# Storing silu's derivative instead of its argument, in the forward pass of a training kernel

## The chip, the cores and the metric

The kernel runs on one core of one Trainium2 chip. The metric is the device time of one execution in microseconds. Three runs of the kernel before gave 873.41, 874.69 and 877.84 us; the median is 874.69 us.

## The reference

One layer of a network and its whole gradient. With B = 1, L = 2048 positions, D = 512 channels, N = 128 states and a hidden width F = 1792, all in bf16:

```python
xn = layernorm(x)
K  = einsum("dn,dnl,dn->dl", C, exp(dt*A*l), dt*B).real     # 2048 taps for each channel
s  = causal_conv(xn, K) + xn * Dskip                        # by FFT in the reference
h  = xn @ w1;  o = silu(h) @ w2                             # 512 -> 1792 -> 512
g  = silu(o)
out = x + s * g
```

The kernel returns `out` and, for a given `grad_out`, the gradients of x, of the six state-space parameters, of log_dt, of Dskip, and of w1 and w2. The two silus matter here. The backward needs their derivatives: the gradient that reaches o is `grad_out * s * silu'(o)`, and the gradient that reaches h is `(do @ w2^T) * silu'(h)`.

## The kernel before

The program is written out by hand in six stages. Each engine works through its own instructions in the order in which the Python code issues them, so the order on ScalarE (ACT) is what the code says, and one instruction that waits holds up all behind it.

**Stage 1** (up to about 197 us) does the forward feed-forward part, and beside it builds tables for the convolution and powers of the state matrix. The generator `gen_ffn_fwd` runs over four groups of 512 positions (`tc_`), and in each over seven pairs of column blocks of w1 (`f0`), 28 steps in all. A step computes two 128x512 blocks of h into a PSUM tile `ps_h` (8 matmuls, L557), and ACT reads that tile twice: once for silu(h) into `aT` (L559), once for a plain copy of h as bf16 into `hs` (L560), which goes to DRAM as `hTd`. The PSUM pool that holds `ps_h` (`pd`) has two buffers, shared with another matmul result (`ps_m`). The previous group's second product is interleaved: `gen_o` accumulates o in `ps_o` (L533) for one block of 128 positions at a time, 16 in all, and for each ACT stores silu(o) into `g2` and a copy of o into `o2` (both through the helper `later`, so the profile shows them on its line, L76). They go to DRAM as `gd` and `od`. In the same steps, from a hand-made list of ticks, ACT computes `Abs` and `Sin` for the transform tables (`tb_w`, `tb_f`, L374 to L378) and for the powers (`b_w`, `b_s`, L465 to L467), and copies PSUM results (`tb_m`, `tb_i`, `XNT`). Near the end of the stage ACT copies the powers into place (`X`, `Y`, `CY`, L720) once they have come back from DRAM as `XYc`.

**Stages 2 to 5** build the kernel K, transform it, do the convolution and its gradient, and the gradients of w2 and of the parameters. In stages 3 and 4, `YOut` loads `od`, `gd`, x and grad_out for two blocks of 128 positions at a time. `pre` applies silu's derivative to the loaded o in place, by the helper `DSILU` (ACT, L133), and multiplies grad_out by it (VectorE, DVE, L1173). `out` then forms the output and the gradient `DO`.

**Stage 6** (from about 680 us) is the feed-forward part's backward. `Bwd.dh` runs over 28 steps. It loads a pair of h blocks (`hsb`, three buffers, asked for three steps ahead), computes silu's derivative of them on ACT into `sd` (L133), eight matmuls of the gradient (`ps_da`, L1626), and on DVE the product of both into `dhT` (L1627). Transposes of `dhT` (L1648), copied out by ACT (L1650), go to DRAM for w1's gradient. `dx` does the second product (L1665) and the layer norm's gradient one step behind.

ACT evaluates functions from tables. The built program has an instruction that loads a table set where the next function isn't in the set that is loaded (`ACT_TABLE_LOAD` in the profile). Before, there are four in the whole program: for exp at the start, for silu at the first L559, for silu's derivative at the first use of L133, and for exp in the last stage. The copies, `Abs` and `Sin` of stage 1 run under silu's set without a load of their own.

The places that the change touches are L537 (the copy of o in `gen_o`), L560, L1172 (in `pre`) and L1620 to L1627 (in `dh`).

Of the kernel before, what the change touches and what calls it, by code (L numbers as in the profile page):

```python
# [9 lines left out]
ALU = mybir.AluOpType  # L10
F32 = mybir.dt.float32
BF16 = mybir.dt.bfloat16
I32 = mybir.dt.int32
AX = mybir.AxisListType
P = 128
# [51 lines left out]
def later(k, fn, *a, **kw):  # L67

    k.after.append((fn, a, kw))


def settle(k):

    todo, k.after = k.after, []
    for fn, a, kw in todo:
        fn(*a, **kw)  # L76
# [55 lines left out]
def DSILU(nc, pool, out, in_):  # L132
    nc.scalar.activation(out=out, in_=in_, func=ACT.Derivative_silu)  # L133
# [364 lines left out]
def gen_ffn_fwd(k, fs, W1, W2):  # L498

    nc = k.nc  # L500

    def xnt(tc_):
        XNT = fs.tile([P, DK, 4, P], BF16, name="XNT", tag="XNT")
        for h in range(2):
            pt = k.ps.tile([P, 2, 4, P], BF16, name="pt_x", tag="ps")
            for d_ in range(2):
                for t in range(4):
                    dk = 2 * h + d_
                    nc.tensor.transpose(out=pt[:, d_, t, :], in_=k.xn[:, 4 * tc_ + t, dk * P:(dk + 1) * P], identity=k.ident[:])
            (nc.scalar.copy if h else nc.vector.tensor_copy)(out=XNT[:, 2 * h:2 * h + 2], in_=pt[:])  # L510
        return XNT

    def trans(tc_, aT, f0):
        pt = k.ps.tile([P, 2, 4, P], BF16, name="pt_a", tag="ps")
        for j in range(2):
            for t in range(4):
                nc.tensor.transpose(out=pt[:, j, t, :], in_=aT[:, f0 + j, t * P:(t + 1) * P], identity=k.ident[:])
        ak = fs.tile([P, 2, 4, P], BF16, name="ak", tag="ak", bufs=3)
        later(k, nc.vector.tensor_copy, out=ak[:], in_=pt[:])
        later(k, nc.sync.dma_start, k.akd[f0:f0 + 2, :, 4 * tc_:4 * tc_ + 4].rearrange("f p t q -> p f t q"), ak[:])  # L520

    def gen_o(tc_, aT):
        for th in range(2):
            ts_ = slice(4 * tc_ + 2 * th, 4 * tc_ + 2 * th + 2)
            g2 = fs.tile([P, 2, D], BF16, name="g2", tag="g2", bufs=1)
            o2 = fs.tile([P, 2, D], BF16, name="o2", tag="o2", bufs=1)
            G2 = fs.tile([P, 2, D], BF16, name="G2", tag="G2", bufs=1)
            nc.sync.dma_start(G2[:], k.g_v[:, ts_, :])
            for t in range(2):
                tt = 2 * th + t  # L530
                pso = k.ps.tile([P, D], F32, name="ps_o", tag="ps")
                for ft in range(FT):
                    nc.tensor.matmul(out=pso[:], lhsT=aT[:, ft, tt * P:(tt + 1) * P], rhs=W2[:, ft, :], start=(ft == 0), stop=(ft == FT - 1))  # L533
                    if ft == FT // 2 - 1:
                        yield
                later(k, nc.scalar.activation, out=g2[:, t, :], in_=pso[:], func=ACT.Silu)
                later(k, nc.scalar.copy, out=o2[:, t, :], in_=pso[:])  # L537
                if t == 0:
                    yield
            later(k, nc.sync.dma_start, k.tl(k.gd[:])[:, ts_, :], g2[:])  # L540
            later(k, nc.sync.dma_start, k.tl(k.od[:])[:, ts_, :], o2[:])
            later(k, later, k, nc.vector.tensor_tensor, out=k.DS[:, ts_, :], in0=G2[:], in1=g2[:], op=ALU.mult)
            yield

    prev = iter(())
    XNT = xnt(0)
    late = None
    for tc_ in range(4):
        aT = fs.tile([P, FT, 512], BF16, name="aT", tag="aT")
        nxt = None  # L550
        for f0 in range(0, FT, 2):
            yield
            ps = k.pd.tile([P, 2, 512], F32, name="ps_h", tag="pd")
            for j in range(2):
                ft = f0 + j
                for dk in range(DK):
                    nc.tensor.matmul(out=ps[:, j], lhsT=W1[:, dk, ft * P:(ft + 1) * P], rhs=XNT[:, dk], start=(dk == 0), stop=(dk == DK - 1))  # L557
            hs = fs.tile([P, 2, 512], BF16, name="hs", tag="hs", bufs=3)
            nc.scalar.activation(out=aT[:, f0:f0 + 2, :], in_=ps[:], func=ACT.Silu)  # L559
            nc.scalar.copy(out=hs[:], in_=ps[:])  # L560
            nc.sync.dma_start(k.hTd[tc_][:, f0:f0 + 2], hs[:])
            next(prev, None)
            if f0 == FT - 2:
                next(prev, None)
            k.mid()
            if late:
                trans(*late)
            late = (tc_, aT, f0)
            if f0 == FT - 4 and tc_ < 3:
                settle(k)  # L570
                nxt = xnt(tc_ + 1)
        XNT = nxt
        prev = gen_o(tc_, aT)
    yield
    trans(*late)
    k.last_aT = aT
    for _ in prev:
        k.mid()
        yield
# [13 lines left out]
def stage_1(k):  # L593
# [14 lines left out]
    su.norm(0)  # L608
    k.mid = lambda: None
    gf = gen_ffn_fwd(k, fs, W1, W2)  # L610
    early = {1: lambda: (su.stats(1), su.norm(1)), 2: lambda: su.param(1), 3: lambda: (su.stats(2), su.norm(2)),
             4: lambda: (su.param(2), su.param(3)), 5: lambda: (su.stats(3), su.norm(3)), 6: lambda: (su.param(4), su.param(5))}
# [538 lines left out]
class YOut:  # L1151
# [17 lines left out]
    def pre(self, t0):  # L1169

        k, nc, r = self.k, self.k.nc, self.ins[t0]
        DSILU(nc, k.y2, r["co"][:], r["co"][:])  # L1172
        nc.vector.tensor_tensor(out=r["cG"][:], in0=r["cG"][:], in1=r["co"][:], op=ALU.mult)  # L1173

    def out(self, t0, S_s):
# [414 lines left out]
class Bwd:  # L1590
# [23 lines left out]
    def dh(self, n):  # L1614
        k, nc = self.k, self.k.nc
        tc_, f0 = n // 7, 2 * (n % 7)
        if f0 == 0:
            self.dhT = self.fb.tile([P, FT, 512], BF16, name="dhT", tag="dhT")
        hs = self.hs.pop(n)
        sd = self.fw.tile([P, 2, 512], BF16, name="sd", tag="sd")  # L1620
        DSILU(nc, self.fw, sd[:], hs[:])
        ps = k.pd.tile([P, 2, 512], F32, name="ps_da", tag="pd")
        for j in range(2):
            ft = f0 + j
            for dk in range(DK):
                nc.tensor.matmul(out=ps[:, j], lhsT=self.W2T[:, dk, ft * P:(ft + 1) * P], rhs=self.DOT[tc_][:, dk], start=(dk == 0), stop=(dk == DK - 1))  # L1626
        nc.vector.tensor_tensor(out=self.dhT[:, f0:f0 + 2, :], in0=ps[:], in1=sd[:], op=ALU.mult)  # L1627
        if n + 3 < 28:
            self.ld_h(n + 3)
        self.trans()  # L1630
        self.late = (tc_, self.dhT, f0)
# [161 lines left out]
```

## Time and profile before

| what | us |
|---|---|
| median of three runs | 874.69 |
| the profiled execution | 874.37 |
| its span in the trace | 872.6 |
| PE (matmuls) busy | 676.4 (78%) |
| DVE busy | 632.0 (72%) |
| ACT busy | 450.6 (52%) |
| POOL busy | 47.6 (5%) |

The times of instructions in the text are from the start of that span. A group of instructions is named by its line, engine, operation and tiles ("out<-in"); "idle before" is the time that the engine stood still just before such an instruction, and the name behind the arrow is what ended it. The chain is the sequence of work and waits that ended last, followed back from the end. The share of busy time is an average over stages that have different limits, so the text reads stretches of the span one by one.

### The profile page before, as it was taken

The numbers are of one execution on the slowest core, as the hardware profiler recorded it, in microseconds if no ns is written. First come the engines' busy times: TensorE is split into PE (matmuls) and PEld (weight loads), VectorE is DVE, ScalarE is ACT, GpSimd is POOL, SyncE is SP. The second block draws the span as 40 slices with busy tenths as digits, with TensorE's granted clock in tenths as the row PEclk, the third lists the DMA queues.
The fourth block names the chain that finished last, engine by engine and source line by source line (L and its number), as shares of the span: only waits on it lengthen the run. The fifth ranks groups of instructions, "written<-read, shape, count | busy, mean of one in ns | idle before, by whom it ended". The sixth has DMA issues, their size and how long they took to land.

```text
span 872.6 us, 13569 instructions
## 1 busy us (share of the span) xinstructions
PE 676.4 (78%) x5213; PEld 346.3 (40%) x5284; DVE 632.0 (72%) x1005; ACT 450.6 (52%) x547; POOL 47.6 (5%) x49
## 2 busy tenths in 40 slices
PE   5677886957557739766879399598688699999966
PEld 2334443423445536322334144243233355555433
DVE  6898888757999962997988999266264347776850
ACT  4459999854879835342444022054244376664231
POOL 1254221000000000000000001000000000000000
PEclk9988997987868859998989799799898899999988
DMA  9547767777769677784788685999879595668362
GB/s 273 175 149 242 266 223 257 264 250 211 217 221 305 187 195 251 266 337 148 259 333 279 209 330 209 253 250 248 208 187 205 146 224 165 177 187 277 98 202 67
DMA packets 183952, 195.18 MB, mean 224 GB/s; under 512 B 35659, under 2 KB 147791, under 8 KB 178767
## 3 DMA queue, kind: packets, MB, share of 16 engines
q1 hardware_dynamic: 179310, 185.53, 69.6%
q10 hardware_dynamic: 4577, 8.77, 3.4%
q8 instruction: 41, 0.67, 0.3%
q14 instruction: 24, 0.20, 0.1%
HBM read 110.10 MB, written 80.50 MB: 218 GB/s over the span
## 4 chain that ended last, share of the span: by engine, by line
PE 36%; DVE 28%; DMA 16%; ACT 9%; issue 6%; SPq 3%; POOL 0%; ACTq 0%; DVEq 0%; POOLq 0%
PE ps_v L1038 7%; DMA XTl<-XTd 5%; PE ps_da L1626 5%; PE ps_dx L1665 4%; PE ps_f L1014 4%; PE ps_w L1744 2%; PE ps_h L557 2%; DMA AW<-akd 2%; PE ps_w L1381 2%; DMA out_dram<-o10b 2%; DVE cm_t L106 2%; PE ps_o L533 1%; PE pt_dh L1648 1%; DVE m L747 1%; PE ps_f L894 1%
## 5 line engine op out<-in xcount | busy, mean ns | idle before, releaser
L1038 PEld LDWEIGHTS <-TIs 128*128 128x128 bf16 x384 | 39.7, 104 | 85.0 <-issue 37.8
L557 PE MATMUL ps_h<-XNT,W 128*128 128x512 bf16 x212 | 61.1, 432 | 14.7 <-ACT hs L560 13.7
L1744 PE MATMUL ps_w<-dhc,xn 128*128 128x448 bf16 x256 | 53.5, 371 | 6.9 <-ACT o10b L1746 6.9
L1531 DVE TENSOR_TENSOR T<-Vb,YTl 128x2048 bf16<-128x2048 bf16 x16 | 19.6, 1225 | 53.5 <-ACT Vb L1522 53.4
L1627 DVE TENSOR_TENSOR dhT<-ps_da,sd 128x1024 bf16<-128x1024 f32 x28 | 34.2, 1224 | 32.7 <-ACT sd L133 19.3
L1014 PEld LDWEIGHTS <-TFs 128*128 128x128 bf16 x336 | 32.9, 100 | 62.0 <-DMA TFs<-TFd 15.4
L1626 PE MATMUL ps_da<-DOT,W2T 128*128 128x512 bf16 x218 | 53.3, 384 | 2.3 <-ACT DOT L1606 1.9
L533 PE MATMUL ps_o<-W,aT 128*128 128x512 bf16 x221 | 53.1, 386 | 0.2
L1381 PE MATMUL ps_w<-DO_all,AW 128*128 128x512 bf16 x212 | 51.5, 388 | 1.9 <-issue 1.8
L1665 PE MATMUL ps_dx<-W1T,dhT 128*128 128x512 bf16 x215 | 52.0, 379 | 0.4
L855 ACT COPY XT<-pt_xt 128x1024 bf16<-128x1024 bf16 (+1 forms) x44 | 41.2, 1010 | 21.5 <-DMA K_b<-Kud 10.1
L1014 PE MATMUL ps_f<-DS,TFs 128*128 128x512 bf16 x173 | 43.3, 400 | 11.2 <-DMA TFs<-TFd 9.5
L894 PE MATMUL ps_f<-xn,TFs 128*128 128x512 bf16 x120 | 36.5, 456 | 16.9 <-ACT XU L895 15.8
L853 PE MATMUL pt_xt<-ident_bfloat,X 128*128 128x128 bf16 x328 | 29.9, 251 | 23.0 <-ACT XT L855 13.4
L1522 ACT CAST Vb<-ps_V 128x1024 bf16<-128x1024 f32 x32 | 31.7, 1013 | 28.9 <-PE ps_V L1520 21.8
L1038 PE MATMUL ps_v<-BG,TIs 128*128 128x512 bf16 x123 | 34.5, 436 | 11.9 <-DMA TIs<-TId 9.4
L1014 PE MATMUL ps_f<-K_b,TFs 128*128 128x512 bf16 x156 | 36.5, 379 | 8.8 <-ACT Ak L1016 5.1
L1038 PE MATMUL ps_v<-BK,TIs 128*128 128x512 bf16 x126 | 31.5, 404 | 13.6 <-DVE BK L97 13.5
L1744 PEld LDWEIGHTS <-xn 128*128 128x128 bf16 x256 | 26.1, 102 | 37.6 <-issue 11.1
L557 PEld LDWEIGHTS <-W 128*128 128x128 bf16 x224 | 23.3, 108 | 41.0 <-issue 25.4
L853 PEld LDWEIGHTS <-X 128*128 128x128 bf16 x328 | 25.3, 114 | 27.2 <-issue 25.4
L452 POOL TENSOR_TENSOR ex<-ex 128x512 f32<-128x512 f32 x21 | 33.0, 1582 | 53.1 <-DVE XYg L480 28.1
(287 smaller groups left out, 1457.9 us busy)
## 6 DMA issues: line engine op xcount, KB each, us to landing
TFs<-TFd SPq DMA_DIRECT2D x12, 1024.0 KB
TIs<-TId SPq DMA_DIRECT2D x24, 512.0 KB
XTd<-XT SPq DMA_DIRECT2D x20, 512.0 KB
XTl<-XTd SPq DMA_DIRECT2D x16, 640.0 KB
UXl<-UXd SPq DMA_DIRECT2D x8, 1024.0 KB
hTd<-hs SPq DMA_DIRECT2D x28, 256.0 KB
akd<-ak SPq DMA_DIRECT2D x28, 256.0 KB
AW<-akd ACTq DMA_DIRECT2D x14, 512.0 KB
```

Source lines behind the costliest of these rows:

```text
L533: nc.tensor.matmul(out=pso[:], lhsT=aT[:, ft, tt * P:(tt + 1) * P], rhs=W2[:, ft, :], start=(ft == 0), stop=(ft == FT - 1))
L557: nc.tensor.matmul(out=ps[:, j], lhsT=W1[:, dk, ft * P:(ft + 1) * P], rhs=XNT[:, dk], start=(dk == 0), stop=(dk == DK - 1))
L853: nc.tensor.transpose(out=pt[:, j, c], in_=X[:, c, P * kk:P * kk + P], identity=k.ident[:])
L855: nc.scalar.copy(out=XT[:, j0:j0 + len(ks)], in_=pt[:, 0:len(ks)])
L894: nc.tensor.matmul(out=ps[:, c, :], lhsT=TFs[:, t1 + 4 * j, c, :], rhs=src[:, t1 + 4 * j, :], start=(j == 0), stop=(j == 3))
L1014: nc.tensor.matmul(out=ps[:, c, :], lhsT=tab(j), rhs=src[:, t1 + 4 * j, :], start=(n == 0), stop=(n == 4 * len(terms) - 1))
L1038: nc.tensor.matmul(out=ps[:, j, :], lhsT=TIs[:, j, 2 * kt + c, :], rhs=B[kt][:, c, (t0 + j) % 4, :], start=(kt == 0 and c == 0), stop=(kt ...
L1381: nc.tensor.matmul(out=ps[:], lhsT=A[:, t, :], rhs=k.DO[:, t, :], start=(t == 0), stop=(t == T - 1))
L1626: nc.tensor.matmul(out=ps[:, j], lhsT=self.W2T[:, dk, ft * P:(ft + 1) * P], rhs=self.DOT[tc_][:, dk], start=(dk == 0), stop=(dk == DK - 1))
L1627: nc.vector.tensor_tensor(out=self.dhT[:, f0:f0 + 2, :], in0=ps[:], in1=sd[:], op=ALU.mult)
L1665: nc.tensor.matmul(out=psx[:], lhsT=dhT[:, ft, t % 4 * P:(t % 4 + 1) * P], rhs=self.W1T[:, ft, :], start=(ft == 0), stop=(ft == FT - 1))
L1744: nc.tensor.matmul(out=ps[:], lhsT=k.xn[:, t, dk * P:(dk + 1) * P], rhs=ch[i][:, t, :], start=(t == 0), stop=(t == T - 1))
```

## The change

The forward stores the derivative where it stored the argument. In the 28 steps on h, ACT reads `ps_h` once for silu and once for silu's derivative, and `hTd` then holds silu'(h). In the 16 blocks of o it does the same, and `od` holds silu'(o). The backward loads these and multiplies by them: 28 instructions on ACT in stage 6 and 8 in stages 3 and 4 are gone, with the tile `sd`. Shapes, types, sizes of transfers, buffers and the order of everything else stay as they were.

In the built program silu and its derivative are in different table sets, and so a load stands ahead of every silu and of every derivative in stage 1: there are 90 `ACT_TABLE_LOAD`s in place of 4. `Abs`, `Sin` and the copies run under either set and need none.

```diff
                 later(k, nc.scalar.activation, out=g2[:, t, :], in_=pso[:], func=ACT.Silu)
-                later(k, nc.scalar.copy, out=o2[:, t, :], in_=pso[:])
+                later(k, DSILU, nc, fs, o2[:, t, :], pso[:])
...
             nc.scalar.activation(out=aT[:, f0:f0 + 2, :], in_=ps[:], func=ACT.Silu)
-            nc.scalar.copy(out=hs[:], in_=ps[:])
+            DSILU(nc, fs, hs[:], ps[:])
...
         k, nc, r = self.k, self.k.nc, self.ins[t0]
-        DSILU(nc, k.y2, r["co"][:], r["co"][:])
         nc.vector.tensor_tensor(out=r["cG"][:], in0=r["cG"][:], in1=r["co"][:], op=ALU.mult)
...
         hs = self.hs.pop(n)
-        sd = self.fw.tile([P, 2, 512], BF16, name="sd", tag="sd")
-        DSILU(nc, self.fw, sd[:], hs[:])
...
-        nc.vector.tensor_tensor(out=self.dhT[:, f0:f0 + 2, :], in0=ps[:], in1=sd[:], op=ALU.mult)
+        nc.vector.tensor_tensor(out=self.dhT[:, f0:f0 + 2, :], in0=ps[:], in1=hs[:], op=ALU.mult)
```

## The prediction

> **What bounds the kernel now.** The change touches ACT in stage 1 (it adds work there) and in stages 3, 4 and 6 (it takes work away). I first asked the stretches of stage 1 how busy each engine is. The stage runs from the first silu at 16.41 us to the first copy of the next stage at 197.03 us.
>
> ```profile
> core 0: us, PE busy (x) PEld busy (x) DVE busy (x) ACT busy (x) POOL busy (x), PEclk, DMA share, GB/s
> 16.41:40.40 23.99, 16.71 (x125) 9.57 (x126) 19.05 (x47) 12.49 (x14) 6.33 (x10) 0.93 0.65 212
> 40.40:64.34 23.94, 19.01 (x116) 10.10 (x117) 23.56 (x50) 14.81 (x19) 10.98 (x7) 0.85 0.41 143
> 64.34:174.66 110.32, 89.08 (x582) 47.81 (x593) 93.20 (x114) 102.47 (x128) 23.50 (x19) 0.92 0.72 248
> 174.66:197.03 22.37, 11.99 (x55) 5.39 (x55) 11.95 (x21) 13.71 (x19) 0.00 (x0) 0.86 0.79 251
> 16.41:197.03 180.62, 136.80 (x874) 72.88 (x889) 147.76 (x229) 143.47 (x178) 40.81 (x35) 0.91 0.68 230
> ```
>
> ACT is free for 37.15 of 180.62 us, but for 7.85 of 110.32 us in the long third stretch: there ACT is the fullest engine, and what is added to it lengthens the stage. In the second stretch DVE is the full one (23.56 of 23.94). The share of ACT over the whole span, 52%, hides this.
>
> The groups of instructions on ACT give the prices, and the timeline shows how a table load stands between two instructions:
>
> ```profile
> L133 ACT ACTIVATE sd<-hsb 128x1024 bf16<-128x1024 bf16 x28 | 29.3, 1050 | 8.0 <-DMA hsb<-hTd 8.0
> L559 ACT ACTIVATE aT<-ps_h 128x1024 bf16<-128x1024 f32 x28 | 29.1, 1040 | 12.5 <-PE ps_h L557 12.3
> L560 ACT CAST hs<-ps_h 128x1024 bf16<-128x1024 f32 x28 | 28.9, 1032 | 2.3 <-DMA hTd<-hs 2.3
> L76 ACT CAST o<-ps_o 128x512 bf16<-128x512 f32 x16 | 10.1, 632 | 0.0
> L559 ACT ACT_TABLE_LOAD x1 | 1.3, 1283 | 0.0
> ```
>
> ```profile
> 381.27 1.93 ACT L1016 CAST Ak<-ps_f 128x1024 bf16<-128x1024 f32 x2 [7.36 <-DVE KX L1029]
> ...
> 385.98 1.01 ACT L1016 CAST Ak<-ps_f 128x1024 bf16<-128x1024 f32 x1 [0.71 <-PE ps_f L1014]
> 387.01 1.28 ACT L133 ACT_TABLE_LOAD   x1
> 388.30 2.00 ACT L133 ACTIVATE co<-co 128x1024 bf16<-128x1024 bf16 x2
> ```
>
> The load starts only when the instruction ahead has ended (385.98 + 1.01 = 386.99), and the next starts when the load has ended. Without a load, two such instructions overlap: two Ak copies take 1.93 us together, so the second starts 0.92 us after the first. From the start of the Ak copy to the start of co it is 2.32 us. One switch costs 2.32 - 0.92 = **1.40 us**. The record is 1283 ns for each of the four loads of the trace, also at 13.62 us, where the DMA share is 0.90 (0 to 20 us).
>
> Last, the chain that ended last, for what the backward can give back:
>
> ```profile
> 690.73 1.06 ACT sd L133
> ...
> 732.71 1.04 ACT sd L133
> ...
> 761.41 1.04 ACT sd L133
> ```
>
> Only 3 of the 28 derivatives of stage 6 lie on the chain. Between them it runs over PE, which is busy for 19.5 to 19.9 of every 20 us from 720 to 820 us.
>
> **Step 1: the table loads in stage 1.** The 44 pairs (28 on h, 16 on o) need 88 loads; the first is there before. So 87 are added: 87 x 1.40 = 121.8 us of ACT time. How much of it goes into ACT's idle time, by stretch:
>
> *16.41 to 40.40.* Six pairs with 11 added loads (15.4 us). A pair took 1.83 us (16.41 to 18.34 less the wait) and takes 4.63, so the sixth silu starts at 39.6 and its derivative ends at 42.9. The copy of XNT follows, ends at 43.9, and releases the transposes that PE started at 33.90 behind that copy. PE then makes the seventh ps_h, in 1.9 (full clock) to 3.4 us (as at 36.94). The seventh silu starts at about 47.1 in place of 40.40: 6.7 us late. Its load lies in that wait.
>
> *40.40 to 64.34.* DVE comes late by the same 7.3 us (its copies of the transposed parameters, at 37.19, wait for PE) and is dense up to 51.8, where it releases b_s (L466): now at 59.1. ACT gets there at 57.8, with silu and derivative 7 and 8 and three loads. After it come two pairs on h and one on o with six loads, and L465 starts at about 75.9 in place of 64.34: **11.5 us late**. DVE has b_f ready at 71 to 72, so from here ACT leads.
>
> *64.34 to 174.66.* 18 pairs on h and 11 on o and the next silu: 59 loads, 82.6 us. Of the 7.85 us of idle time 5.55 are waits for DVE and PE, which stay within what ACT now needs; I count them as gone. The last 2.30 are a wait of g for its store (`DMA gd<-g`). The load for that g carries the wait in the program, so only the load and the rest of o ahead of it cover 1.4 of it. Late by 11.5 + 82.6 - 5.55 - 1.4 = 87.2 us.
>
> *174.66 to 197.03.* Seven loads (9.8 us). ACT waited 5.34 us for XYc, whose loads stand in SP's queue behind the stores gd and od, which wait for ACT. XYc comes 87.2 us later, ACT is at that place 87.2 + 4.2, so 4.2 are covered and X starts 87.2 late. The wait of 3.29 before the g at 190.69 is for stores behind XYc in SP's queue and stays. The last four loads add 5.6. The stage ends **92.7 us late**: 121.8 less 29 of the 37.15 us of idle time. From there on each engine and queue is late by the same, as XYl, the next load on the chain, is asked for behind that od.
>
> Bounds: all idle time used up gives 121.8 - 37.2 = 85; only half of it 103. PE is made late too: it waits more, and the granted clock is low where PE is less busy (0.77 from 180 to 200 us, 1.00 from 80 to 120). A step's PE work (ps_h, half a ps_o, transposes: some 5 us) fits into the 9 us that ACT then needs, so I add nothing, and 10 us to the upper end.
>
> **Step 2: derivative for copy.** 28 x (1050 - 1032) ns = 0.5 us on h, read from PSUM where the row has SBUF; silu from PSUM is 1040. On o, g's 643 against 632 ns. Under 1 us; in the bounds. Reading `ps_h` longer delays its buffer, which PE needs again two tiles later; ACT's queue covers that as above. The stores of hs and o2 are the same size, asked for by SP in the same order.
>
> **Step 3: the backward.** Gone: 28 x 1.05 = 29.4 us and 8 x 1.06 = 8.4 us of ACT, and the load at 387.01. On the path: at 690.73 the product waits for the DMA of hsb alone, 1.06 sooner; at 732.71 and 761.41 sd stood ahead of the copy that frees PE's buffer: 1.04 each. That is 3.1. DVE's other waits for sd (19.3 us in 16 places, 9.0 of them the first) are off the path, since PE is the bound. In stages 3 and 4 the derivative held ACT's queue for the DMA of co (19.2 us in 3 places); PE waited 0.7 us for the S_s behind it. At 387 PE waited for DMA TFs. Now DVE's cG waits for co itself; it stands late in DVE's order (447.34 against co's landing at 442.5; 471.64 against 465.0), so that wait is nil, and would hold up only DO and the radix steps behind it. I take 4.0 in all, bounds 3 to 6.
>
> **The sum** against the profiled execution: 872.6 + 92.7 - 4.0 = 961.3 us of span; 1.8 lie around it (874.37 - 872.6): 963. That execution is 0.3 below the median of the runs, so nothing is added for that.
>
> A rule speaks against this change: the Trainium skill (ScalarE: Activation LUTs, What ACT_TABLE_LOAD costs, and Table sets: the hidden batching unit) says to batch calls by table set, and puts a switch at 1283 ns for the load and some 1380 ns for a drain, 2.66 us in all. The trace agrees with the first number; between Ak and co there is no room for the second.
>
> **Rivals.**
> *A, ACT leads and takes up most of its idle time*: 963, from 952 (all idle time, 6 given back) to 975 (half of it). Chance 0.80.
> *B, PE's slower clock and the two PSUM buffers make new waits*, so that little idle time is used: 121.8 - 9 + 1 - 3 more than 872.6, 985; up to 995. For it speaks 0.80 at 60 to 80 us, where PE and ACT already take turns (5.50 us of PE's wait for hs at 69.25). Chance 0.13.
> *C, a switch costs twice as much when sets alternate* (a gap as long as the load's own 1.28 beside it, which the four single loads don't show): 87 x (1.40 + 1.28) = 233 less 37 and 4, so 1066. Against it: 0.02 us between the end of Ak and the load, 0.01 after it. Chance 0.03. By the rule of that page it would be 87 x 2.66 = 231 in place of 233, so 1064.
> *D, not slower*: a load that runs ahead while ACT still works, or a set that stays. Then stage 1 hides it, and 4 are gained: 870. It decides where 87 loads fit into the 29 us that stage 1 covers and the 4 given back: under 0.38 us each. The load at 13.62 does run while ACT would wait for PE anyway; but behind a silu there is no such wait, and the four records are 1.28. Chance 0.04, of which half is faster by over 0.5% (0.5% is about what a measurement of this kernel can tell). That the loads aren't there at all is excluded by the built program, which has them.
>
> **Range.** 8 in 10 holds A with its bounds and the nearer part of B: 949 to 985.
>
> **What would show it.** In the changed kernel's groups, L559, L133 and L76 with 28 + 28 + 16 + 16 loads, less any that line up otherwise, of 1283 ns each; ACT busy for over 95% from 75 us to the end of stage 1, which ends near 290 us; the stretch from there to stage 6 as long as before within 2 us; the product L1627 no longer waiting for ACT; stage 6 some 3 us shorter. I am wrong if loads are shorter or overlap (D), if ACT shows idle time between load and silu waiting for PE in most steps (B), or if a gap stands ahead of each load (C).

## The result, and the profile after

The changed kernel takes 963.1 us (median of four runs, 961.63 to 969.84) beside 876.14 us for the kernel before (four runs, 873.41 to 877.84): a ratio of 1.101 with an interval of 1.097 to 1.106, so about 88 us or 10% slower. The execution in the trace took 961.63 us, its span is 959.8 us.

The stretches of stage 1 in the changed kernel, cut at the same five events as those shown of before (first silu, seventh silu, L465, the g that was at 174.66, first copy of stage 2), with the same columns:

```profile
core 0: us, PE busy (x) PEld busy (x) DVE busy (x) ACT busy (x) POOL busy (x), PEclk, DMA share, GB/s
15.63:44.56 28.93, 18.20 (x137) 9.99 (x139) 21.15 (x55) 28.58 (x25) 6.56 (x10) 1.00 0.58 183
44.56:71.85 27.29, 15.66 (x84) 7.33 (x84) 24.35 (x48) 27.05 (x28) 15.80 (x10) 0.89 0.34 118
71.85:258.45 186.60, 107.27 (x603) 55.74 (x614) 89.96 (x112) 183.98 (x187) 17.60 (x15) 0.75 0.43 148
258.45:286.03 27.58, 11.42 (x53) 5.10 (x52) 13.63 (x25) 23.13 (x25) 0.00 (x0) 0.78 0.66 207
15.63:286.03 270.40, 152.55 (x874) 78.16 (x889) 149.10 (x237) 262.74 (x264) 39.96 (x35) 0.79 0.46 155
```

The stage ends at 286.03 us in place of 197.03: 89.0 us later. ACT is busy for 262.74 of 270.40 us (before 143.47 of 180.62), and for 183.98 of 186.60 in the third stretch. Of its 37.15 us of idle time 7.66 are left, so 29.5 were used. ACT works 119.27 us more for 87 added loads, which is 1.37 us for each.

The groups on ACT in that stage of the changed kernel (count, busy us, mean ns, idle before):

```profile
L133 ACT ACT_TABLE_LOAD x44 | 56.5, 1283 | 0.8
L559 ACT ACT_TABLE_LOAD x27 | 34.6, 1283 | 0.5
L559 ACT ACTIVATE aT<-ps_h 128x1024 bf16<-128x1024 f32 x28 | 28.6, 1023 | 1.6 <-PE ps_h L557 1.3
L133 ACT ACTIVATE hs<-ps_h 128x1024 bf16<-128x1024 f32 x28 | 28.6, 1023 | 0.3
L76 ACT ACT_TABLE_LOAD x16 | 20.5, 1283 | 3.5 <-DMA gd<-g 3.2
```

Every load takes 1283 ns, as each of the four did before, and silu waits for PE's ps_h for 1.3 us in all 28 steps (12.3 before). The derivative that is read from PSUM takes 1023 ns, the same as silu. ACT's timeline shows the spacing:

```profile
20.30 1.02 ACT L559 ACTIVATE aT<-ps_h 128x1024 bf16<-128x1024 f32 x1
21.35 1.28 ACT L133 ACT_TABLE_LOAD   x1
22.64 1.02 ACT L133 ACTIVATE hs<-ps_h 128x1024 bf16<-128x1024 f32 x1
23.68 1.28 ACT L559 ACT_TABLE_LOAD   x1
24.98 1.02 ACT L559 ACTIVATE aT<-ps_h 128x1024 bf16<-128x1024 f32 x1
```

The load starts 0.02 to 0.03 us after the end of the instruction ahead, the function 0.01 us after the load. A pair takes 4.68 us from silu to silu; the prediction had 4.63.

PE, on the other side, now stands and waits. Its group for ps_h in the page of the changed kernel, and then the same group in the page of the kernel before:

```profile
L557 PE MATMUL ps_h<-XNT,W 128*128 128x512 bf16 x212 | 65.6, 455 | 58.4 <-ACT hs L133 56.3
```

```profile
L557 PE MATMUL ps_h<-XNT,W 128*128 128x512 bf16 x212 | 61.1, 432 | 14.7 <-ACT hs L560 13.7
```

PE waits 56.3 us, in place of 13.7, for ACT to have read a buffer. The side that waits shows which one is the bound.

What follows stage 1 nearly keeps its length: from the first copy of stage 2 to the end of the span it is 675.6 us before and 673.8 after. In the backward the product takes what it waited for from elsewhere (the group in the page of the changed kernel, then in that of the kernel before):

```profile
L1624 DVE TENSOR_TENSOR dhT<-ps_da,hsb 128x1024 bf16<-128x1024 f32 x28 | 34.1, 1221 | 31.0 <-PE ps_da L1623 23.6
```

```profile
L1627 DVE TENSOR_TENSOR dhT<-ps_da,sd 128x1024 bf16<-128x1024 f32 x28 | 34.2, 1224 | 32.7 <-ACT sd L133 19.3
```

DVE's 19.3 us of waiting for sd are gone, and its idle time there fell by 1.7 us only: it waits for PE's `ps_da` (23.6 us) and for the load of `hsb` instead.

### The profile page after: what moved, and what is told of

Its sections match the earlier page's. It is cut to its first block, busy times and chain, and to the rows that moved or that the text cites. A ratio compares the mean times of both kernels' runs of the same rounds, so it can differ in the third digit from the quotient of the medians.

```text
span 959.8 us, 13597 instructions
## 1 busy us (share of the span) xinstructions
PE 688.2 (72%) x5213; PEld 350.3 (36%) x5284; DVE 629.7 (66%) x1005; ACT 535.0 (56%) x597; POOL 46.2 (5%) x49
## 4 chain that ended last, share of the span: by engine, by line
PE 26%; DVE 14%; DMA 13%; ACT 3%; issue 2%; SPq 2%; ACTq 0%; DVEq 0%
PE ps_da L1623 5%; PE ps_dx L1662 4%; DMA XTl<-XTd 4%; PE ps_f L1014 4%; PE ps_v L1038 3%; PE ps_w L1741 3%; PE ps_w L1380 3%; DMA AW<-akd 3%; DVE cm_t L106 2%; DMA out_dram<-o10b 1%; PE pt_dh L1645 1%; DMA TIs<-TId 1%; PE ps_V L1519 1%; DVE cm_t L108 1%; DVE cm_t L107 1%
## 5 line engine op out<-in xcount | busy, mean ns | idle before, releaser
L557 PE MATMUL ps_h<-XNT,W 128*128 128x512 bf16 x212 | 65.6, 455 | 58.4 <-ACT hs L133 56.3
L133 ACT ACT_TABLE_LOAD x44 | 56.5, 1283 | 0.8
L533 PE MATMUL ps_o<-W,aT 128*128 128x512 bf16 x221 | 55.9, 400 | 0.2
L1624 DVE TENSOR_TENSOR dhT<-ps_da,hsb 128x1024 bf16<-128x1024 f32 x28 | 34.1, 1221 | 31.0 <-PE ps_da L1623 23.6
L1530 DVE TENSOR_TENSOR T<-Vb,YTl 128x2048 bf16<-128x2048 bf16 x16 | 19.6, 1224 | 53.1 <-ACT Vb L1521 52.9
L1647 ACT COPY dhk<-pt_dh 128x1024 bf16<-128x1024 bf16 x28 | 28.1, 1002 | 42.8 <-PE pt_dh L1645 23.1
L76 DVE COPY ak<-pt_a 128x1024 bf16<-128x1024 bf16 x28 | 19.2, 686 | 38.0 <-PE pt_a L517 38.0
```

## The experiments

Theory: a switch costs 1.37 to 1.40 us of ACT time wherever it stands, and the time is what of that stage 1 cannot cover. Its rivals: the other half of the change costs something (the derivative itself, the longer hold of PSUM); the loads cost time by what they do to PE; the gain in the backward is another than thought. Times in microseconds below are (ratio - 1) x 876, with the interval of the ratio carried over.

### The change without its loads

The changed kernel with silu itself in both places, so that both reads of PSUM, all stores and the lighter backward stay, and 87 loads go. Its gradients through silu are not the reference's.

```diff
-                later(k, DSILU, nc, fs, o2[:, t, :], pso[:])
+                later(k, nc.scalar.activation, out=o2[:, t, :], in_=pso[:], func=ACT.Silu)
...
-            DSILU(nc, fs, hs[:], ps[:])
+            nc.scalar.activation(out=hs[:], in_=ps[:], func=ACT.Silu)
```

> The changed kernel with silu in place of its derivative in both places of stage 1 (so hTd and od hold silu, and the gradients are not the reference's): every instruction, buffer and wait stays, but one table set serves all and there are 3 loads in place of 90. Theory (the loads on ACT's queue make the whole difference): 872, between 870 and 874, that is before less what the backward gives back (2 to 4 us). Rival (the second function read from PSUM, or PE's waits for the buffer, cost something themselves): above 877, 5 to 30 us more than before.

Measured: 871.54 us, ratio 0.9958 (0.9930 to 0.9986), 3.7 us less than before (1.2 to 6.1). Its stage 1 in the windows view:

```profile
15.30:193.10 177.80, 135.41 (x890) 72.77 (x889) 148.31 (x232) 143.52 (x177) 42.15 (x35) 0.92 0.70 236
```

ACT is busy for 143.52 us, where the kernel before has 143.47, and PE's clock is 0.92, where it had 0.91. So the activation in place of the copy costs nothing that shows, and all of the loss comes with the loads.

### One switch for each pair in place of two

Every second pair does the derivative first and silu behind it, so the set at the end of one pair is that at the start of the next.

```diff
+def PAIR(k, s, d, in_):
+    k.npair += 1
+    todo = [(s, ACT.Silu), (d, ACT.Derivative_silu)]
+    for out, func in todo if k.npair % 2 else todo[::-1]:
+        k.nc.scalar.activation(out=out, in_=in_, func=func)
...
-            nc.scalar.activation(out=aT[:, f0:f0 + 2, :], in_=ps[:], func=ACT.Silu)
-            DSILU(nc, fs, hs[:], ps[:])
+            PAIR(k, aT[:, f0:f0 + 2, :], hs[:], ps[:])
```

> The changed kernel with the order inside each pair turned round every second time (silu, derivative; derivative, silu; ...), so that one switch and not two falls to a pair: 47 loads in place of 90. Theory (1.40 us of ACT time for each load, of which ACT's idle time takes up some 25 to 29): 44 loads in stage 1 are 61.6 us, so 875 + 61.6 - 27 - 2 = 907, between 900 and 915. Rival (what counts is that two functions alternate at all, or PE's slower clock, not the number of loads): within 10 us of the changed kernel, above 950.

Measured: 918.19 us, ratio 1.050 (1.044 to 1.055): 43.5 us over the kernel before (39 to 48), above the expected 900 to 915. The window of its stage 1, and two lines of its ACT timeline (start, us, and in brackets the idle time ahead and what ended it):

```profile
15.92:239.20 223.28, 150.83 (x890) 76.18 (x889) 147.32 (x231) 203.70 (x222) 41.54 (x35) 0.84 0.56 185
```

```profile
42.61 1.02 ACT L140 ACTIVATE aT<-ps_h 128x1024 bf16<-128x1024 f32 x1 [5.24 <-PE ps_h L563]
...
53.21 1.06 ACT L473 ACTIVATE b_s<-b_f 128x1024 f32<-128x1024 f32 x1 [1.40 <-DVE Ctr L444]
```

The price of a load held: 203.70 - 143.47 = 60.2 us for 44 added loads, 1.37 each. What missed is the cover. I had put 27 us of the idle time down as used; 223.28 - 203.70 = 19.6 are left, so 17.6 were used. With half the loads ACT is not late enough to pass the waits for PE and DVE in the stage's first part (5.24 and 1.40 here), so they stay. How much idle time loads fill depends on where they stand and on how late the engine then is; it is no fixed sum.

The rule of the Trainium skill that the prediction cited, to batch calls by set (ScalarE: Activation LUTs, Table sets: the hidden batching unit), is borne out in direction: half the switches, about half the loss.

### Only h, and only o

The derivative of h stored in the forward with o copied as before (56 added loads), and the other way round (31).

```diff
-                later(k, DSILU, nc, fs, o2[:, t, :], pso[:])
+                later(k, nc.scalar.copy, out=o2[:, t, :], in_=pso[:])
...
+        DSILU(nc, k.y2, r["co"][:], r["co"][:])
```

> Only the 28 pairs on h are changed, o is stored and derived as before: 60 loads. Theory: 56 loads more, 78 us of ACT time, less 26 to 30 that fall into idle time, less 1 in stage 6: 875 + 78 - 28 - 1 = 924, between 918 and 932. Rival (idle time takes up loads in proportion, so 28 of 44 pairs make 28 of 44 parts of the 87 us): 930 exactly would not tell the two apart; below 912 or above 940 both are wrong.

```diff
-            DSILU(nc, fs, hs[:], ps[:])
+            nc.scalar.copy(out=hs[:], in_=ps[:])
...
+        sd = self.fw.tile([P, 2, 512], BF16, name="sd", tag="sd")
+        DSILU(nc, self.fw, sd[:], hs[:])
```

> Only the 16 pairs on o are changed: 34 loads. Theory: 31 loads more in stage 1, 43 us, of which idle time after 55 us can take up 12 to 18: 875 + 43 - 15 - 1 = 902, between 898 and 908; and with the run on h alone the two parts add up to more than or about as much as 87 us less one use of the idle time, that is, their sum is 10 to 20 us below the whole change's, as each uses the same idle time once. Rival (a fixed price for each load whatever is idle): 875 + 43 = 918 or more.

Measured: h alone 926.09 us, ratio 1.059 (1.054 to 1.064), 51.6 us, as expected; o alone 908.39 us, ratio 1.039 (1.034 to 1.044), 34.1 us, just above what was expected. Their stage 1, h alone and then o alone:

```profile
16.60:248.80 232.20, 153.53 (x890) 76.52 (x889) 146.56 (x229) 220.12 (x234) 39.49 (x35) 0.84 0.53 179
```

```profile
15.70:228.90 213.20, 145.21 (x890) 75.30 (x889) 149.31 (x236) 186.18 (x209) 41.60 (x35) 0.85 0.59 196
```

ACT's work is up by 76.65 us for 56 loads and by 42.7 for 31: 1.37 and 1.38 each. The two losses add up to 85.7 us beside 88.7 for the whole. I had expected the sum to lie 10 to 20 below the whole, because both would spend the same idle time. They use 25 and 10 us of it, 35 together, and the whole uses 29.5: the loads of o stand mostly where ACT has no idle time, so the two have little of it in common.

### The same 14 loads in two places

If idle time covers loads, 14 of them in the stage's first part cost less than 14 in its last. The derivative is stored in the forward for seven pairs of h alone, the first seven or the last seven, and the backward of the same seven steps multiplies by what it loads; the rest is as before.

```diff
+            if tc_ == 0:
+                DSILU(nc, fs, hs[:], ps[:])
+            else:
+                nc.scalar.copy(out=hs[:], in_=ps[:])
```

> The kernel before, with the change made only for the first 7 of the 28 pairs on h (up to about 47 us, ahead of and inside the stretches where ACT has 20 us of idle time): 14 more loads, 19.6 us. Theory (idle time takes them up): 0 to 5 us more, 877. Rival (each load adds its price): 894.

> The same 14 loads for the last 7 pairs on h (from about 130 us, where ACT is nearly full). Theory: 19.6 us less the few us of waits there (2.7 + 1.6 + some of the waits for DMA after the last pair): 10 to 17 us more, 888. Rival (place does not matter): as much as the run with the first 7.

Measured: first seven 880.62 us, ratio 1.003 (1.0003 to 1.0058), 2.6 us (0.3 to 5.1); last seven 895.74 us, ratio 1.019 (1.014 to 1.023), 16.3 us (12 to 20). Their stage 1 in the same order:

```profile
16.50:200.70 184.20, 137.49 (x874) 72.23 (x889) 147.41 (x229) 162.35 (x192) 42.22 (x35) 0.92 0.67 225
```

```profile
16.60:215.00 198.40, 142.25 (x874) 74.51 (x889) 148.12 (x229) 163.00 (x192) 41.46 (x35) 0.87 0.62 209
```

ACT does the same work in both (162.35 and 163.00). In the first the idle time falls from 37.15 to 21.85; in the second it stays at 35.40. This is the cleanest pair of the study: about six times the loss for the same number of loads. In the traces stage 1 is 3.6 and 17.8 us longer than before. Each of the two also leaves seven derivatives out of the backward, which is worth far less than this difference (all 36 are worth 2.7 us, below), so the place makes it. The group of silu on ACT in the first, and then in the second, names the wait that takes up the largest part of them (12.5 us before):

```profile
L559 ACT ACTIVATE aT<-ps_h 128x1024 bf16<-128x1024 f32 x28 | 29.1, 1040 | 3.2 <-PE ps_h L557 3.0
```

```profile
L559 ACT ACTIVATE aT<-ps_h 128x1024 bf16<-128x1024 f32 x28 | 29.0, 1036 | 12.6 <-PE ps_h L557 12.4
```

In the first the wait of `b_s` for DVE has shrunk too, from 4.72 us before to 0.24.

### Loads in a stage that has room on ACT

The kernel before, with a tiny silu behind every third step of stage 6 from the tenth on. Each forces two switches; 13 more loads in all.

```diff
+        if n >= 9 and n % 3 == 0:
+            tn = self.fw.tile([P, 1], BF16, name="tn", tag="tn")
+            nc.scalar.activation(out=tn[:], in_=k.rstd[:, 0:1], func=ACT.Silu)
```

> The kernel before, with a silu of one column of rstd (its result is not used) after every third step of stage 6 from the tenth on: 7 small instructions and 13 more loads, 13 x 1.40 + 7 x 0.2 = 19.6 us of ACT time where PE is the bound. Theory (a load costs ACT time, and the kernel only where ACT leads): 0 to 5 us more, 877. Rival (a load stops more than ACT): 15 to 20 us more, 893.

Measured: 884.41 us, ratio 1.007 (1.005 to 1.009), 6.2 us (4 to 8): between the two expectations. Its timeline, all engines, around one load:

```profile
736.43 1.28 ACT L133 ACT_TABLE_LOAD   x1
...
737.73 1.06 ACT L133 ACTIVATE sd<-hsb 128x1024 bf16<-128x1024 bf16 x1
738.69 0.99 ACT L1653 COPY dhk<-pt_dh 128x1024 bf16<-128x1024 bf16 x1
...
739.73 0.61 PE L1605 MATMUL pt_do<-ident_bfloat,DO_all 128*128 128x128 bf16 x8 [1.77 <-ACT dhk L1653]
```

ACT has idle time here, yet the load stands ahead of a derivative and a copy that frees PE's buffer, and PE waits 1.77 us. In the kernel before it waits 0.35 us at this place (734.70), so this load costs PE 1.42 us, its full price. There are two such places (1.77 and 1.71 us). At seven others the late derivative holds up the product on DVE, and PE waits 0.53 to 0.86 us for that product, 4.9 us in all; in the kernel before it has no such wait beyond the first. So loads reach PE at 9 places of this trace, with 7.7 us of new waits, and about a third of the added ACT time (19.6 us with the tiny silus) reaches the end. A low busy share of ACT doesn't make a load free.

### The backward's part alone

The kernel before with the 36 derivatives of the backward left out and nothing in their place.

```diff
-        DSILU(nc, k.y2, r["co"][:], r["co"][:])
...
-        sd = self.fw.tile([P, 2, 512], BF16, name="sd", tag="sd")
-        DSILU(nc, self.fw, sd[:], hs[:])
...
-        nc.vector.tensor_tensor(out=self.dhT[:, f0:f0 + 2, :], in0=ps[:], in1=sd[:], op=ALU.mult)
+        nc.vector.tensor_tensor(out=self.dhT[:, f0:f0 + 2, :], in0=ps[:], in1=hs[:], op=ALU.mult)
```

> Step 3 of the prediction alone. The kernel before, with the 36 derivatives of the backward left out and nothing in their place: the products take the loaded h and o themselves (so all gradients that pass through silu are not the reference's), the forward is untouched, 3 table loads. Theory (the prediction's step 3): 4.0 us less than before, 872 (3 to 6 less): 3.1 of it in stage 6, 0.7 in stage 4. Rival (the chain's pieces of 1.04 us at the two later derivatives stand for waits of PE of only 0.35 us each): some 2.5 us less or under, 873.5 to 875. Second rival (nothing of it was on the path): no change, 876.

Measured: 872.99 us, ratio 0.9969 (0.9949 to 0.9990), 2.7 us less (0.9 to 4.5). The products of stage 6 in the tile view (ns least, median, most; first and last start in us), for this kernel and then for the kernel before:

```profile
L1624 DVE TENSOR_TENSOR dhT<-ps_da,hsb x28: 1215/1224/1225, 692.4 to 791.7; 128x1024 bf16<-128x1024 f32 x28
```

```profile
L1627 DVE TENSOR_TENSOR dhT<-ps_da,sd x28: 1214/1224/1225, 691.8 to 791.2; 128x1024 bf16<-128x1024 f32 x28
```

From first to last product it is 99.3 us without the derivatives and 99.4 with them, so the two later pieces of 1.04 us on the chain, which the prediction counted in full, don't show in this length. It isn't fine enough to price them: in the kernel with o alone, which has the same loop as the kernel before, it is 100.4 us. What they were worth is read from PE's waits, in the part on step 3 below.

### Can the kernel before take its part of that gain?

The kernel before with each derivative of stage 6 issued at the end of the step ahead, so that none stands in front of the next copy of transposes.

```diff
-        sd = self.fw.tile([P, 2, 512], BF16, name="sd", tag="sd")
-        DSILU(nc, self.fw, sd[:], hs[:])
+        sd = self.sd.pop(n)
...
         self.trans()
+        if n + 1 < 28:
+            self.ds(n + 1)
```

> The whole computation of the kernel before. In stage 6 the derivative sd of a step is issued at the end of the step before, behind the copies of the transposes, so that the next copy of transposes has no derivative ahead of it; 4 table loads, as before. If the derivative's place in ACT's queue is what costs stage 6 its part of step 3, 1 to 3 us less than before: 873 to 875. Rival (a derivative that is issued a step earlier waits for the load of its h block, which then arrives later than ACT gets there, and holds up the copies): 0 to 4 us more, 876 to 880.

Measured: 878.31 us, ratio 1.0024 (0.9993 to 1.0054): no gain, and no loss that is told from none. The tile view of its products:

```profile
L1628 DVE TENSOR_TENSOR dhT<-ps_da,sd x28: 1215/1224/1226, 694.0 to 794.7; 128x1024 bf16<-128x1024 f32 x28
its engine sat idle before it (us, times) until:
  PE ps_da L1627: 21.7, 11
  DVE dhT L1628: 13.7, 2
  ACT sd L133: 12.9, 5
```

DVE's waits for sd fell from 19.3 to 12.9 us, and the products take 100.7 us in place of 99.4 (100.4 with o alone), so the loop is no shorter. PE's timeline shows why: its two waits of 0.35 us for the copy `dhk` are gone, but at 711.35 it waits 2.07 us for ACT's copy `DOT`, where it waited 1.12 us before. ACT now does the next step's derivative at 709.34, ahead of that copy. The derivative has moved from one copy's way into another's, and neither rival of the expectation named this. With the derivatives gone altogether the whole program gains 2.7 us (0.9 to 4.5), so another place for them in the backward has little to gain; none of the versions measured here beats the kernel before while computing all that it computes.

## Why the prediction was right, point by point

**ACT is the bound of stage 1, and what is added there lengthens it (rival A).** Right: the loss is in that stage (+89.0 us to its end), ACT is full there, and without the loads the loss is gone.

**Price of a switch: 1.40 us, from one load beside the Ak copies.** Right to 2%: 1.37 us of ACT time for each of the 87, and 1.37, 1.37 and 1.38 in the kernels with 44, 56 and 31. With 14 loads the difference is too small to read it as closely: 1.35 and 1.40. The drain of some 1380 ns that the Trainium skill adds (ScalarE: Activation LUTs, What ACT_TABLE_LOAD costs) isn't there: an estimate from that page's 2.66 us for a switch is 87 x 2.66 = 231 us of ACT time, and the measured addition is 119.3. Of the Trainium skill's two numbers there, 1283 ns is what each of the records shows. The gaps of 0.01 to 0.03 us rule out rival C as well.

**29 of 37.15 us of idle time used.** Measured 29.5. By stretch the step was less exact:

| stretch, up to | predicted late | measured late |
|---|---|---|
| seventh silu | 6.7 | 4.2 |
| L465 | 11.5 | 7.5 |
| g of 174.66 | 87.2 | 83.8 |
| X copies | 87.2 | 83.8 |
| end of stage | 92.7 | 89.0 |

The miss of 4.0 us stands in the first two stretches; from L465 to the end of the stage it is +81.5 us measured beside +81.2 predicted. Of the 4.0, 0.8 is only that the first silu starts at 15.63 us in this execution, and at 16.41 in that of the kernel before. The terms at fault are two waits, the first that for the seventh silu (2.5 of the 4.0, with the 0.8). I had PE's transposes of the parameters wait for ACT's copy of XNT, as before. PE's timeline before, and after:

```profile
33.90 0.38 PE L336 MATMUL pt_par<-ident_bfloat,nat 128*128 128x128 bf16 x4 [1.59 <-ACT XNT L510]
...
36.94 3.42 PE L557 MATMUL ps_h<-XNT,W 128*128 128x512 bf16 x8
```

```profile
38.83 0.38 PE L336 MATMUL pt_par<-ident_bfloat,nat 128*128 128x128 bf16 x4 [1.92 <-DVE ak L76]
39.42 0.38 PE L336 MATMUL pt_par<-ident_bfloat,nat 128*128 128x128 bf16 x4 [0.21 <-DVE XNT L510]
39.64 1.89 PE L557 MATMUL ps_h<-XNT,W 128*128 128x512 bf16 x8
```

After, both wait for DVE, and the ps_h behind them is made in 1.89 us from 39.64 on, where I had ACT's copy end at 43.9. I had taken the buffer that each transpose waits for as fixed, and it is not. In each of the eleven traces the two transposes wait for the two copies out of the pool `ps` (three buffers) that end first. In the kernel before ACT's copy of XNT ends first of the three, at 33.85 us; in the changed kernel DVE's two copies end at 38.77 and 39.37, ahead of ACT's at 43.25. How the build comes to choose so was not tried.

The second wait at fault is that of b_s for DVE at 59.1, from which the second stretch was worked out: DVE's `Ctr`, which releases b_s, ends at 53.95 us, 2.1 later than before and not 7.3, so that wait is gone as well, and ACT leads from there on.

**The wait of g for its store stays.** Right. From ACT's timeline of the changed kernel:

```profile
268.93 2.27 ACT L720 COPY X<-XYc 128x2048 bf16<-128x2048 bf16 x2 [1.20 <-DMA XYc<-XYd]
274.23 1.28 ACT L76 ACT_TABLE_LOAD   x1 [3.04 <-DMA gd<-g]
275.53 0.60 ACT L76 ACTIVATE g<-ps_o 128x512 bf16<-128x512 f32 x1
```

XYc is waited for 1.20 us (5.34 before; predicted 1.1), the store 3.04 us (3.29 before, where the trace names DVE's X at L749 as what ended it). The wait stands on the load, which starts only behind it, so the load comes on top. Where ACT waits for PE's `ps_h`, it is otherwise: at 125.23 us the load runs at once, and the silu behind it then waits 0.54 us.

**PE's slower clock makes ACT wait no more than before (against rival B).** Right, and against what the clock suggested: PE's granted clock fell from 0.91 to 0.79 over the stage, and ACT's wait for ps_h fell from 12.3 to 1.3 us. PE had room enough in a step to be slower.

**Step 2, under 1 us.** Right: the two activations from PSUM are both 1023 ns, and the kernel without loads has ACT's busy time unchanged.

**Step 3, 4.0 us given back.** The term was too large: the backward's part alone measured 2.7 us (0.9 to 4.5), below the stated 3 to 6, though 4.0 itself lies within the measured interval; the single pair of traces shows 1.8 (675.6 to 673.8). The part that failed is two of the three pieces of the chain. The piece of 1.06 us at 690.73 went as described: the first product of the changed kernel, at 778.81, waits for the DMA of hsb and no longer for ACT; what that gained was not measured by itself. The two of 1.04 us were counted at their own length, and that is not what they held up. In the timeline of the kernel before, PE's wait behind the first of them is short:

```profile
732.71 1.04 ACT L133 ACTIVATE sd<-hsb 128x1024 bf16<-128x1024 bf16 x1
733.66 0.99 ACT L1650 COPY dhk<-pt_dh 128x1024 bf16<-128x1024 bf16 x1
...
734.70 0.61 PE L1605 MATMUL pt_do<-ident_bfloat,DO_all 128*128 128x128 bf16 x8 [0.35 <-ACT dhk L1650]
```

The second, at 763.40, is as short. PE's waits of this kind in the kernel before (total us, times, longest):

```profile
PE pt_do L1605 <- ACT dhk L1650: 0.7, 2, 0.3
```

In the changed kernel, and in the four others here whose backward has no derivative on h, PE has no such wait; in the kernel with o alone, which keeps these derivatives, it is 0.7 us again. A piece on the chain tells how long the work took, not how much sooner the next could have run: each of the two was worth 0.35 us. PE's wait of 0.7 us for S_s in stage 4 is gone too. With these terms step 3 comes to 1.06 + 0.7 + 0.7, some 2.5 us, which agrees with the 2.7 measured. "Stage 6 some 3 us shorter" was wrong for the same reason: its product loop is 99.4 us long before and 99.4 after (778.8 to 878.2). The stretch between stage 1 and stage 6 is as long as before within 2 us, as said (494.8 and 492.8 us from the first copy of stage 2 to the first product).

That the sum came out at 963 beside 963.1 is partly luck. The two misses have opposite signs: 3.7 us too much in stage 1, 2.2 too much given back by the pair of traces. What they leave, 1.5 us, is made up by chance: the execution in the trace, with 961.63 us, lies that far below the median. The lower bound of rival A, 952, leaves out the 1.8 us around the span; by its own terms it is 953.

## What to carry to other kernels

Price a table switch by its load (about 1.4 us of ACT time here) times the number of changes between sets in ACT's program order, and then ask stretch by stretch whether ACT has a wait at that place that the load can fill; 14 loads cost 2.6 us in one place and 16.3 in another. Moving a function to where its input already lies is no saving when its neighbour there lives in another table set: 36 derivatives in the backward were worth 2.7 us, and the 87 loads that their move brought made stage 1 end 89 us later. On a chain, take the wait of the next engine as the price of a piece (0.35 us here), and not the piece's own length (1.04).

## What was not expected of the hardware

PE's granted clock went with how busy it was, and not only in the mean: 0.92 in the third stretch before, with PE busy for 89.08 of 110.32 us, and 0.75 after, with 107.27 of 186.60. Over the whole of stage 1 it was 0.91 before, 0.92 with 14 loads early, 0.87 with 14 late, 0.84 to 0.85 with 31 to 56, and 0.79 after. No cost of it shows here, since ACT set the pace. In the first stretch, though, it was 1.00 with PE busy for 18.20 of 28.93 us (0.93 with 16.71 of 23.99 before), so the busy share alone doesn't give it; the runs don't settle what does.
